# A feed-forward layer whose first tokens are loaded in another order: transposes of 1, 2 and 2 contraction tiles, all issued ahead of the start barrier

## Chip, cores and metric

The kernel runs on one core of a Trainium2 chip. The metric is the device time of one execution in microseconds (us); lower is better. Times are given as the median of several runs; a profile is one further execution, taken by the hardware profiler. All times below are in us unless marked otherwise, and times inside an execution count from its first instruction.

## What is computed

```
B, S, D, F = 1, 2048, 640, 1728          # x, w1, w2 in bf16
h = jnp.einsum("bsd,df->bsf", x, w1)     # contraction over D
h = silu(h)
out = jnp.einsum("bsf,fd->bsd", h, w2)   # contraction over F
```

## The kernel before

Tokens are worked in four chunks of 512 (`SCH`). D = 640 is five contraction tiles of 128 (`DT`), and F = 1728 is 13 blocks of 128 (`FT`) and one of 64. TensorE needs x with the contraction on the partitions, so x comes from memory by DMA transposes into `xT`; a transpose moves one or more contraction tiles of one chunk (`turned`, line 90, named T(k) or T(k,k+1) below after its tiles). w1 comes by plain DMAs into `w1s`. For the first eight blocks (1024 columns), they are slabs: slab k holds contraction tile k (`slab`, line 118, 256 KB). Slab 0 is split: its first five blocks are issued by ScalarE, the rest by SyncE. The remaining columns of w1 are two more DMAs (lines 151 and 152).

The first chunk is worked with the contraction outermost, so that work can begin when only a part of x and w1 is there. The eight PSUM banks hold eight blocks, and a sweep k (`sweep`, line 189) adds contraction tile k to all eight. A block of a sweep is two matmuls of 64 columns (`step`, line 180), which run side by side; below they are called a pair. Sweep k waits for slab k and for the transpose that brings tile k. With sweep 4 (line 207) the banks close one by one and ScalarE applies Silu to each. Then come blocks 8 to 12 of the first chunk, then the other three chunks, then the second product, and the stores. Those later stages are not touched.

Ahead of the real work TensorE runs dummy matmuls on a zeroed tile (`first_dummies`, line 135): 13 of 128 columns and one pair of 64, each over 256 columns.

Each engine starts with a barrier: it announces its arrival, then waits for the others. The helper `early` (line 98) takes instructions out of the place where they were written and puts them ahead of that barrier: with `arrived=False` ahead of the engine's own arrival, otherwise between its arrival and its wait. So what SyncE issues early delays its arrival, and with it what the others do behind their waits. In the kernel before, SyncE issues T(0,1), the rest of slab 0, slabs 1 and 2 and T(2) ahead of its arrival, and slab 3, T(3,4), slab 4, the rest of w1 and the 15 transposes of the later chunks (line 160) behind the barrier. TensorE runs the dummies and sweeps 0 and 1 (`opening`, line 194) between its arrival and its wait. Behind the barrier stand ScalarE's load of the Silu table with a warming activation (line 154) and GpSimd's memset for it (line 141).

SyncE issues everything in the order of the text, on one queue; ScalarE has a queue of its own for its part of slab 0.

Of the kernel before, what the change touches and what calls it, by code (L numbers as in the profile page):

```python
# [9 lines left out]
def bass_standalone__dense_activation_silu__prompt_kernel(  # L10
# [13 lines left out]
    P = 128  # L24
    NB = 8
    BANK = 512
    DT = D // P
    FT = F // P
    FL = F - FT * P
    SCH = 512  # L30
# [8 lines left out]
    pe, act, dve, pool, sp = nc.tensor, nc.scalar, nc.vector, nc.gpsimd, nc.sync  # L39

    with ExitStack() as es:
# [18 lines left out]
        def sem(name):  # L60
            s = es.enter_context(nc.semaphore(name))
            count[s.name if hasattr(s, "name") else name] = 0
            return [s, 0]

        def tick(ins, s, n=1):
            ins.then_inc(s[0], n)
            s[1] += n
            return (s, s[1])

        def wait(eng, *points):  # L70
            for pt in points:
                if pt is None:
                    continue
                s, v = pt
                key = (id(eng), id(s))
                if seen.get(key, 0) < v:
                    eng.wait_ge(s[0], v)
                    seen[key] = v
# [6 lines left out]
        def load(eng, out_ap, in_ap):  # L85
            s = sem(f"s_ld{n_dma[0]}")
            n_dma[0] += 1
            return tick(eng.dma_start(out=out_ap, in_=in_ap), s, 16)

        def turned(c0, c1, k0, k1):  # L90
            s = sem(f"s_tr{n_dma[0]}")
            n_dma[0] += 1
            return tick(sp.dma_start_transpose(
                out=xT[:, k0:k1, c0:c1], in_=xf[c0:c1, k0 * P:k1 * P]), s, 16)

        ET = mybir.EngineType

        def early(emit, engine, arrived=True):
            n = len(nc.main_func.blocks[0].instructions)
            r = emit()  # L100
            lst = nc.main_func.blocks[0].instructions
            new = lst[n:]
            del lst[n:]
            at = next(
                i for i, ins in enumerate(lst)
                if ins.opcode == ("EventSemaphore" if arrived else "Drain") and ins.engine == engine
            )
            lst[at:at] = new
            return r
# [8 lines left out]
        def slab(eng, k, f0=0, f1=NO):  # L118
            return load(eng, w1s[:, k, f0 * P:f1 * P], w1_v[:, k, f0 * P:f1 * P])

        ld_w1 = {}
        ld_t = {}
        ld_t[0] = ld_t[1] = early(lambda: turned(0, SCH, 0, 2), ET.SP, False)
        ld_w1[0] = early(lambda: slab(act, 0, 0, NA), ET.Activation, False)
        p_z = early(lambda: tick(dve.memset(z[:, :], 0.0), s_dve), ET.DVE, False)  # L125

# [2 lines left out]
        def dummies(n, w):  # L129
            for _ in range(n):  # L130
                for c0 in range(0, P, w):
                    pe.matmul(ps[c0:c0 + w, 3, 0:HB], lhsT=z[:, 0:w], rhs=z[:, :],  # L132
                              start=True, stop=True)

        def first_dummies():
            wait(pe, p_z)
            dummies(13, P)
            dummies(1, HC)


        p_warm = tick(pool.memset(warm[:, :], 0.0), s_pool)  # L141

        ld_w1b = early(lambda: slab(sp, 0, NA, NO), ET.SP, False)
        ld_w1[1] = early(lambda: slab(sp, 1), ET.SP, False)
        ld_w1[2] = early(lambda: slab(sp, 2), ET.SP, False)
        ld_t[2] = early(lambda: turned(0, SCH, 2, 3), ET.SP, False)
        ld_w1[3] = slab(sp, 3)
        ld_t[3] = ld_t[4] = turned(0, SCH, 3, DT)
        ld_w1[4] = slab(sp, 4)
        CM = CO + 2 * P  # L150
        ld_rest = load(sp, w1s[:, :, CO:CM], w1_v[:, :, CO:CM])
        ld_rest2 = load(sp, w1s[:, :, CM:F], w1_v[:, :, CM:F])
# [33 lines left out]
        def part(k, ft, c0, c1, start=False, stop=False):  # L186
            return step(ft, k, ft, c0, c1, start, stop)

        def sweep(k, c0, c1, *waits):
            wait(pe, *waits)  # L190
            for ft in range(NO):
                part(k, ft, c0, c1)

        def opening():
            first_dummies()
            wait(pe, ld_t[0], ld_w1[0])
            for ft in range(NO):
                if ft == NA:
                    wait(pe, ld_w1b)
                part(0, ft, 0, SCH, start=True)  # L200
            sweep(1, 0, SCH, ld_w1[1], ld_t[1])

        early(opening, ET.PE)
        for k in range(2, DT - 1):
            sweep(k, 0, SCH, ld_w1[k], ld_t[k])
        wait(pe, ld_w1[4], ld_t[4])
        for ft in range(NO):
# [202 lines left out]
```

## Time and profile before

| | us |
|---|---|
| median of 3 runs | 125.18 |
| lowest, highest | 124.72, 125.32 |
| the profiled execution's own time | 124.39 |
| its span, first to last instruction | 122.9 |
| TensorE busy in the span | 120.4 |
| ScalarE busy | 38.8 |
| VectorE busy | 6.9 |

A line of the profile names a source line (L172 is the helper that issues every real matmul, L132 the dummies), an engine (PE is a TensorE matmul, PEld its weight load, SPq the issuing of a DMA by SyncE), and the tiles written and read. In the order of time, the first two numbers are the start and the length of a group, x the number of instructions in it, and the brackets give the idle time before it and what ended it. The length of a DMA line is only the time that the engine takes to issue it; the DMA view gives the time from issue to landing. Durations of pipelined matmuls overlap: their rate is read from the spacing of their starts.

### The profile page before, as it was taken

To read this page: it belongs to the slowest core of one execution; us is meant where nothing else is said; L and a number is where in the kernel's file an instruction comes from. 1 tells how busy PE (TensorE), PEld (TensorE's weight loads), DVE (VectorE), ACT (ScalarE), POOL (GpSimd) and SP (SyncE) were. 2 spreads that over 40 slices of the span, in tenths; PEclk is the share of its full clock that TensorE was granted. 3 is DMA by queue.
4 is the path that set the end of the run, shared out by engine and by line. 5 is a ranking of instruction groups with operands and counts; after the bars stand their busy time and mean duration, and the time that the engine had idled before them with its cause. 6 is when DMAs were issued, how large, how long until landed. Compare 5 with 4: busy or idle time off the path is not lost.

```text
span 122.9 us, 2298 instructions
## 1 busy us (share of the span) xinstructions
PE 120.4 (98%) x1056; PEld 58.9 (48%) x1057; DVE 6.9 (6%) x11; ACT 38.8 (32%) x67; POOL 0.3 (0%) x5
## 2 busy tenths in 40 slices
PE   8999999999999999999999999999999999999993
PEld 5455555555555555555544444444444444444452
DVE  0000000000000000000000022002101300222001
ACT  0403975555555555555530011002101200110110
POOL 0000000000000000000000000000000000000000
PEclk9999999999999999999999999999999999999999
DMA  7999955465991000000000014202200220022122
GB/s 150 242 217 341 135 122 116 92 84 100 303 392 43 0 0 0 8 0 0 0 0 5 0 25 103 48 0 107 107 0 5 107 107 0 5 107 107 53 75 85
DMA packets 19481, 10.42 MB, mean 85 GB/s; under 512 B 13456, under 2 KB 18960, under 8 KB 19472
## 3 DMA queue, kind: packets, MB, share of 16 engines
q1 hardware_dynamic: 19184, 10.05, 32.3%
q10 hardware_dynamic: 288, 0.23, 0.7%
q8 instruction: 8, 0.13, 0.4%
q14 instruction: 1, 0.01, 0.0%
HBM read 4.51 MB, written 2.62 MB: 58 GB/s over the span
## 4 chain that ended last, share of the span: by engine, by line
PE 98%; issue 0%; ACT 0%; DVEq 0%
PE ps L172 95%; PE ps L132 3%; ACT o_sb L254 0%; DVEq L395 0%
## 5 line engine op out<-in xcount | busy, mean ns | idle before, releaser
L172 PE MATMUL ps<-xT,w1s 128*64 128x512 bf16 x540 | 58.9, 381 | 0.0
L172 PE MATMUL ps<-w2s,hT 64*128 64x512 bf16 (+3 forms) x376 | 46.0, 369 | 0.2 <-issue 0.2
L172 PEld LDWEIGHTS ps<-xT,w1s 128*64 128x64 bf16 x540 | 30.0, 111 | 28.6 <-issue 0.5
L176 ACT ACTIVATE hT<-ps 128x512 bf16<-128x512 f32 x52 | 30.0, 608 | 24.7 <-PE ps L172 24.7
L172 PEld LDWEIGHTS ps<-w2s,hT 64*128 64x128 bf16 (+1 forms) x377 | 21.0, 95 | 24.1 <-issue 0.2
L254 ACT CAST o_sb<-ps 128x512 bf16<-128x512 f32 (+1 forms) x9 | 4.9, 550 | 41.5 <-PE ps L172 41.5
L172 PE MATMUL ps<-hT,w2s 64*128 64x512 bf16 x104 | 11.7, 376 | 0.0
L172 PEld LDWEIGHTS ps<-hT,w2s 64*128 64x128 bf16 x104 | 5.0, 94 | 6.3 <-issue 0.4
L252 DVE CAST o_sb<-ps 128x512 bf16<-128x512 f32 (+1 forms) x8 | 5.4, 674 | 40.5 <-PE ps L172 40.5
L252 DVE CAST oT<-ps 128x512 bf16<-128x512 f32 x2 | 1.4, 692 | 73.3 <-PE ps L172 73.3
L254 ACT CAST oT<-ps 128x512 bf16<-128x512 f32 x2 | 1.2, 585 | 10.6 <-PE ps L172 10.6
L132 PE MATMUL ps<-z 128*128 128x256 bf16 (+1 forms) x15 | 3.3, 419 | 0.4 <-DVE z L125 0.4
L172 PE MATMUL ps<-w2t,hTt 64*128 64x512 bf16 (+2 forms) x17 | 2.9, 364 | 0.0
L154 ACT ACT_TABLE_LOAD x1 | 1.3, 1283 | 4.8 <-DVEq L395 4.8
L132 PEld LDWEIGHTS ps<-z 128*128 128x128 bf16 (+1 forms) x15 | 1.9, 143 | 1.5 <-issue 0.4
L176 ACT ACTIVATE hTt<-ps 128x512 bf16<-128x512 f32 x2 | 1.2, 597 | 1.0 <-PE ps L172 1.0
L172 PEld LDWEIGHTS ps<-w2t,hTt 64*128 64x128 bf16 x17 | 0.9, 94 | 1.1
L172 PE MATMUL ps<-hTt,w2t 64*128 64x512 bf16 x4 | 0.8, 376 | 0.0
L172 PEld LDWEIGHTS ps<-hTt,w2t 64*128 64x128 bf16 x4 | 0.2, 94 | 0.2
L154 ACT ACTIVATE warm<-warm 128x32 f32<-128x32 f32 x1 | 0.2, 229 | 0.0
L125 DVE MEMSET z<- 128x128 uint32 x1 | 0.2, 165 | 0.2 <-issue 0.2
L141 POOL MEMSET warm<- 128x32 f32 x1 | 0.1, 124 | 4.3 <-POOLq L395 4.3
(4 smaller groups left out, 0.4 us busy)
## 6 DMA issues: line engine op xcount, KB each, us to landing
out_dram<-o_sb SPq DMA_DIRECT2D x15, 160.0 KB, 1.8
w2s<-in_w_dram SPq DMA_DIRECT2D x1, 1120.0 KB, 6.4
w1s<-in_w_dram SPq DMA_DIRECT2D x4, 256.0 KB, 3.7
w2s<-in_w_dram SPq DMA_DIRECT2D x1, 960.0 KB, 8.5
w1s<-in_w_dram SPq DMA_DIRECT2D x1, 560.0 KB, 5.4
w1s<-in_w_dram SPq DMA_DIRECT2D x1, 320.0 KB, 4.3
xT<-in_x_dram SPq DMA_TRANSPOSE x18, 3.7
w1s<-in_w_dram ACTq DMA_DIRECT2D x1, 160.0 KB, 2.5
```

The costliest lines, as they stand in the source:

```text
L125: p_z = early(lambda: tick(dve.memset(z[:, :], 0.0), s_dve), ET.DVE, False)
L132: pe.matmul(ps[c0:c0 + w, 3, 0:HB], lhsT=z[:, 0:w], rhs=z[:, :], start=True, stop=True)
L141: p_warm = tick(pool.memset(warm[:, :], 0.0), s_pool)
L154: act.activation(out=warm[:, :], in_=warm[:, :], func=ACT.Silu)
L172: return pe.matmul(o, lhsT=l, rhs=r, start=start, stop=stop, skip_group_check=shared)
L176: r = tick(act.activation(out=out_ap, in_=in_ap, func=ACT.Silu), s_act)
L252: r = tick(dve.tensor_copy(out=out_ap, in_=in_ap), s_dve)
L254: r = tick(act.copy(out=out_ap, in_=in_ap), s_act)
```

## The change

The first transpose brings only tile 0, the second tiles 1 and 2, the third tiles 3 and 4. SyncE issues, all ahead of its arrival: T(0), the rest of slab 0, slab 1, T(1,2), slab 2, T(3,4), slab 3, slab 4. So slab 1 goes ahead of the second transpose, and slab 3 behind the third, where it was ahead of it. TensorE runs sweep 2 too before it waits at the barrier. Of the dummies of 128 columns, 10 are left of 13.

```diff
-        ld_t[0] = ld_t[1] = early(lambda: turned(0, SCH, 0, 2), ET.SP, False)
+        ld_t[0] = early(lambda: turned(0, SCH, 0, 1), ET.SP, False)
...
-            dummies(13, P)
+            dummies(10, P)
             dummies(1, HC)
...
         ld_w1b = early(lambda: slab(sp, 0, NA, NO), ET.SP, False)
         ld_w1[1] = early(lambda: slab(sp, 1), ET.SP, False)
+        ld_t[1] = ld_t[2] = early(lambda: turned(0, SCH, 1, 3), ET.SP, False)
         ld_w1[2] = early(lambda: slab(sp, 2), ET.SP, False)
-        ld_t[2] = early(lambda: turned(0, SCH, 2, 3), ET.SP, False)
-        ld_w1[3] = slab(sp, 3)
-        ld_t[3] = ld_t[4] = turned(0, SCH, 3, DT)
-        ld_w1[4] = slab(sp, 4)
+        ld_t[3] = ld_t[4] = early(lambda: turned(0, SCH, 3, DT), ET.SP, False)
+        ld_w1[3] = early(lambda: slab(sp, 3), ET.SP, False)
+        ld_w1[4] = early(lambda: slab(sp, 4), ET.SP, False)
...
-            sweep(1, 0, SCH, ld_w1[1], ld_t[1])
+            for k in (1, 2):
+                sweep(k, 0, SCH, ld_w1[k], ld_t[k])
 
         early(opening, ET.PE)
-        for k in range(2, DT - 1):
+        for k in range(3, DT - 1):
             sweep(k, 0, SCH, ld_w1[k], ld_t[k])
```

## The prediction

> **What bounds the kernel now.** I read the engine totals first, then the chain that ended last, then the opening in order of time, for SyncE and for TensorE, and last the DMA view over short windows.
>
> ```profile
> PE 120.4 (98%) x1056; PEld 58.9 (48%) x1057; DVE 6.9 (6%) x11; ACT 38.8 (32%) x67; POOL 0.3 (0%) x5
> ...
> PE 98%; issue 0%; ACT 0%; DVEq 0%
> PE ps L172 95%; PE ps L132 3%; ACT o_sb L254 0%; DVEq L395 0%
> ```
>
> TensorE is the chain from end to end: L132 are the dummies, L172 all real matmuls. Behind the opening it never idles, so the end moves by exactly what moves in the opening. The opening in order of time (start, length, engine, in brackets the idle time before and what ended it):
>
> ```profile
> 0.00 1.33 SPq L93 DMA_TRANSPOSE xT<-in_x_dram  x1
> 1.39 1.51 SPq L88 DMA_DIRECT2D w1s<-in_w_dram  x3
> 2.94 1.16 SPq L93 DMA_TRANSPOSE xT<-in_x_dram  x1
> 4.75 0.33 SPq L88 DMA_DIRECT2D w1s<-in_w_dram  x1
> 5.14 1.24 SPq L93 DMA_TRANSPOSE xT<-in_x_dram  x1
> 6.43 1.62 SPq L88 DMA_DIRECT2D w1s<-in_w_dram  x3
> ...
> 0.39 3.31 PE L132 MATMUL ps<-z 128*128 128x256 bf16 x15 [0.39 <-DVE z L125]
> 3.60 0.18 PEld L172 LDWEIGHTS ps<-xT,w1s 128*64 128x64 bf16 x4 [0.20 <-DMA xT<-in_x_dram]
> ...
> 3.60 1.03 PE L172 MATMUL ps<-xT,w1s 128*64 128x512 bf16 x4
> ...
> 4.46 0.60 PE L172 MATMUL ps<-xT,w1s 128*64 128x512 bf16 x4
> ...
> 9.65 10.52 PE L172 MATMUL ps<-xT,w1s 128*64 128x512 bf16 x96
> ```
>
> Real work starts at 3.60, when the first transpose lands. Its first two pairs (the two 64-column halves of a block run together) start at 3.60 and 4.03, the next at 4.46 and 4.68: 0.43 each, then 0.216 (the last row: 48 pairs, (10.52 - 0.38)/47). The clock step lies at about 4.46; only this spacing shows it, as the page's row of granted clock is full from the first slice. So a sweep of 8 pairs costs 1.73, and the sweeps start at 3.60; 4.46 + 6 x 0.216 = 5.76; 7.48; 9.21; 10.94. The first Silu at 11.37 is one matmul after the last of these, so there is no hidden stall.
>
> The landings, issue plus the DMA view's time to landing: T(0,1) 3.6, slab 0's rest 1.39 + 3.6 = 4.99, slab 1 2.01 + 3.6 = 5.61, slab 2 2.47 + 3.8 = 6.27, T(2) 2.94 + 3.9 = 6.84, slab 3 4.75 + 2.8 = 7.55, T(3,4) 5.14 + 3.5 = 8.64, slab 4 6.43 + 3.9 = 10.33. Each is ahead of its sweep, by 0.15 (slab 1) to 0.6.
>
> Why slab 3 took 2.8 and slab 4 3.9 is in the DMA rows. GB/s from 2.8 to 4.4, behind T(0,1); from 7.8 to 9.8, behind T(3,4); from 5.8 to 7.0, behind the single T(2):
>
> ```profile
> GB/s 238 212 225 199 147 192 134 20 58 19 90 58 51 0 0 38 38 19 58 58 96 205 218 154 423 179 294 192 141 154 0 173 70 192 90 365 243 480 224 531
> ...
> GB/s 292 308 308 174 200 118 87 0 82 41 123 82 164 41 123 123 82 123 123 164 174 143 102 195 205 246 123 154 184 215 184 410 215 410 348 358 348 215 348 348
> ...
> GB/s 256 213 86 179 154 60 119 111 34 248 179 171 102 359 154 17 290 154 77 341 273 273 341 205 478 68 410 137 273 341 273 410 478 410 410 273 546 341 171 265
> ```
>
> Behind a two-tile transpose the queue crawls for about a microsecond; behind the single one it is soon at 300 and more. In landings: slab 4 lands 10.33 - 8.64 = 1.7 after the two-tile T(3,4); slab 0's rest and slab 1 land 1.4 and 2.0 after T(0,1); slab 3 lands 0.7 after the single T(2). Data arrive in the order of issue throughout.
>
> **The change, part by part.** First the issue times, with the durations and gaps of before. A single-tile transpose costs 1.16 against 1.24, so the first costs 1.33 - 0.08 = 1.25. Then: slab 0's rest 1.31, slab 1 1.93, T(1,2) 2.39, slab 2 3.68, T(3,4) 4.15, slab 3 5.44, slab 4 5.91 to 6.34. SyncE then arrives; before it took 0.65 from its last early issue (4.10) to its next instruction (4.75), so 6.99. The two remaining slabs of w1 (7.00 before) and the 15 later transposes (8.09) keep their times. Cost 0.
>
> *Waits on SyncE's arrival.* ScalarE's table load goes from 4.75 to 6.99, plus 1.28 and 0.23: ready at 8.5, needed at 11.37. GpSimd's memset (0.12) lies inside that. TensorE meets the barrier after sweep 2, at 9.4 or later. All covered, by 2.4 at least; they would cost only if SyncE came later than that.
>
> *Three dummies fewer, a single first tile.* The dummies end 3 x 0.2135 = 0.64 earlier, at 3.70 - 0.64 = 3.06 (the spacing: two dummies of 256 columns equal one cold pair). T(0) carries 128 KB less: 0.47 at some 280 GB/s and 0.08 of issue, so it lands at 3.05 instead of 3.6. Bounds: 2.7, the shortest landing of any transpose in the trace, and 3.6, no gain. Starting at 3.05, 1.41 is cold: 3.28 pairs, and 4.72 x 0.216 = 1.02 follow. Sweep 0 ends at 5.48, **0.28 ahead** of before. Slab 0's rest is due by 4.8 and comes 0.7 to 1.4 after T(0): hidden.
>
> *T(1,2), due at 5.48.* Before, tiles 0 and 1 came together. Now tile 1 is issued at 2.39 in a two-tile transpose, whose landing took 3.6 and 3.5. It lands at 5.95 (5.9 to 6.3 by the three early rows; slab 1 ahead of it lands 1.3 to 2.0 after T(0), at 4.35 to 5.05, and a two-tile transpose 1.09 after the slab ahead, worked out below: no later than 6.14). Sweep 1 waits 0.47 and starts at 5.95: **+0.19** against 5.76. The early start is spent.
>
> *Slab 2, due at 5.95 + 1.73 = 7.68.* It stands behind a two-tile transpose: + 1.7 gives 7.65, just in time; + 0.7 gives 6.65.
>
> *T(3,4), due at 9.41.* A two-tile transpose lands 1.09 after the slab ahead of it (8.64 - 7.55): 8.74. In time.
>
> *Slab 3, due at 9.41 too.* This is the step I choose as the deciding one. Before it was ahead of T(3,4), behind the single tile; now it is behind T(3,4), in the very place of slab 4. Both ends: + 1.7 gives 10.44, a wait of 1.03; + 0.7 on the short chain (6.65, 7.74) gives 8.44, none. I take 1.7, the row of the same bytes behind the same transpose. Sweep 3 starts at 10.44 instead of 9.21: **+1.23**. Slab 4 follows by some 0.66 (as slab 2 follows slab 1): 11.1, due at 12.17. The rest of w1 and the next 512 tokens keep their issue while TensorE is later: hidden.
>
> The sum: 124.39 (the profiled execution) + 1.23 = **125.6**.
>
> Against the median: the three runs lie 0.33 to 0.93 above the profiled one, and the trace can't show where. In the new kernel the start of sweep 3 is set by the loads from SyncE's first instruction on, so time that TensorE loses ahead of it (a later clock step above all) is absorbed, up to the 1.03 of the wait. Since TensorE never idles behind the opening, I put the runs' extra time there: 125.6 holds for the median too, +0.3% on 125.18. [...]
>
> **The rivals.** *Slower: the wait rides on top.* Place: slab 3 ahead of sweep 3. If the runs' extra 0.79 lies behind the opening or in the loads, nothing absorbs it: 125.18 + 1.23 = 126.4. It decides from the point where slab 3 lands over 0.63 behind the moment at which the kernel before starts sweep 3 in the same run (9.84 against 9.21 in the profiled one). For it: the median lies above the profile, the cause unseen. Against: no idle time behind the opening.
>
> *The queue recovers fast.* If slabs 2 and 3 land 0.7 behind their transposes, only T(1,2) is left: +0.19 with the clock step of the profile, down to -0.28 with a later one: about 125.2. For it: slab 3 of before. Against: both two-tile rows.
>
> *The transposes are quick and the early start stays.* If T(1,2) landed like a slab of its size (2.8, slab 3), at 5.19, and the slabs 0.7 behind, all 0.28 would be kept: 124.9; with a clock step after sweep 0 the whole 0.55: 124.6. Against: 3.5, 3.6 and 3.9 for the early transposes. [...]
>
> *The change doesn't start earlier.* T(0) lands at 3.6 all the same, and TensorE idles from 3.06. That would cost nothing more, since sweep 1 waits for T(1,2).
>
> **How the numbers follow.** The forecast 0.37 (its own range 125.2 to 126.0), with the last rival in it; on top 0.33; fast recovery 0.20; quick transposes 0.10. A measurement of this kernel tells about 0.5% from no change, 0.63 either way: 124.55 to 125.81. Faster is only the far end of the quick case: 0.06. Slower: the case on top and the upper edge of the forecast, 0.38. The same: 0.56. The range from 124.8 to 126.6 leaves out the far ends.
>
> **What would show it.** Right: real matmuls from about 3.05, a wait before sweep 1 for xT until about 5.95, and one before sweep 3 for w1s until about 10.4, with GB/s near 100 for a microsecond behind each two-tile transpose. Wrong: slab 3 landing before 9.4, T(1,2) before 5.5, or the clock step much later than 4.46.

## The result, and the profile after

The changed kernel takes 125.40 us (median of 22 runs, 124.99 to 126.11) against 124.84 (22 runs, 124.45 to 125.37) for the kernel before: a ratio of 1.0047, with a 95% interval of 1.0033 to 1.0062. It is 0.5% slower, just inside the band that the prediction calls the same. The new kernel's profiled execution took 126.11, the longest of its 22; that of before, 124.39, lies below all of its 22 (from 124.45). So the two profiles lie further apart (1.72) than the medians (0.56). The ratios leave out runs more than 1.5% above the fastest of their kernel: 2 of 12 in e10 and 6 of 13 in e11, the one profiled among these, and none elsewhere.

The engine totals and the chain that ended last, of the changed kernel:

```profile
PE 121.1 (97%) x1054; PEld 59.6 (48%) x1054; DVE 7.0 (6%) x11; ACT 38.8 (31%) x67; POOL 0.3 (0%) x5
...
PE 90%; SPq 4%; DMA 4%; issue 0%; ACT 0%
PE ps L171 90%; DMA w1s<-in_w_dram 4%; SPq L93 3%; SPq L88 1%; ACT o_sb L254 0%
```

TensorE is no longer the chain from end to end: 8% of it is now SyncE's issuing and one DMA of w1. The later part of the chain in order of time says which (start, length, what):

```profile
4.31 1.24 SPq L93
5.55 0.04 issue
5.59 5.27 DMA w1s<-in_w_dram
10.86 0.04 issue
10.90 111.82 PE ps L171 x993
```

The DMA issued at 5.59 is slab 3, the first copy behind T(3,4). It lands at 10.86, and sweep 3 starts with it. The opening in order of time:

```profile
0.39 2.67 PE L132 MATMUL ps<-z 128*128 128x256 bf16 x12 [0.39 <-DVE z L125]
1.30 1.03 SPq L88 DMA_DIRECT2D w1s<-in_w_dram  x2
2.38 1.26 SPq L93 DMA_TRANSPOSE xT<-in_x_dram  x1
...
3.06 0.18 PEld L171 LDWEIGHTS ps<-xT,w1s 128*64 128x64 bf16 x4 [0.29 <-DMA xT<-in_x_dram]
3.06 6.59 PE L171 MATMUL ps<-xT,w1s 128*64 128x512 bf16 x48
...
4.77 0.18 PEld L171 LDWEIGHTS ps<-xT,w1s 128*64 128x64 bf16 x2 [0.24 <-issue]
5.20 0.33 PEld L171 LDWEIGHTS ps<-xT,w1s 128*64 128x64 bf16 x4 [0.24 <-issue]
...
5.98 0.60 PEld L171 LDWEIGHTS ps<-xT,w1s 128*64 128x64 bf16 x8 [0.46 <-issue]
...
7.05 1.28 ACT L153 ACT_TABLE_LOAD   x1 [7.05 <-DVEq L395]
10.90 0.62 PE L171 MATMUL ps<-xT,w1s 128*64 128x512 bf16 x4 [1.25 <-DMA w1s<-in_w_dram]
```

Real work starts at 3.06 instead of 3.60. The weight loads 0.43 apart (4.77, 5.20) belong to the pairs ahead of what the prediction calls the clock step, "cold" below: the point where the spacing of the pairs falls from 0.43 to 0.216. Here the step comes at 5.2, not at 4.46. As before, only the spacing shows it: the granted clock is 1.00 on both sides of it, in the kernel before (3.60 to 4.46, 4.46 to 9.20) and in the changed one (3.06 to 5.20, 5.20 to 9.65). So "clock" is my reading; what makes the step isn't shown. Sweep 1 starts at 6.01 (5.76 before), sweep 2 at 7.74 (7.49), sweep 3, behind 1.25 of idle time, at 10.90 (9.22).

One number orders all that follows. The time of the profiled execution less the start of sweep 3 is 124.39 - 9.22 = 115.17 before and 126.11 - 10.90 = 115.21 after. In nine of the experiments that have such a pair below it is 115.18 to 115.24 too. So nothing behind the start of sweep 3 costs more or less in these, and a kernel's time can be read as the start of sweep 3 plus 115.2.

### The profile page after: what moved, and what is told of

It reads as the page before. It is cut to its first block, busy times and chain, and to the rows that moved or that the text cites. A ratio compares the mean times of both kernels' runs of the same rounds, so it can differ in the third digit from the quotient of the medians.

```text
span 124.6 us, 2293 instructions
## 1 busy us (share of the span) xinstructions
PE 121.1 (97%) x1054; PEld 59.6 (48%) x1054; DVE 7.0 (6%) x11; ACT 38.8 (31%) x67; POOL 0.3 (0%) x5
## 4 chain that ended last, share of the span: by engine, by line
PE 90%; SPq 4%; DMA 4%; issue 0%; ACT 0%
PE ps L171 90%; DMA w1s<-in_w_dram 4%; SPq L93 3%; SPq L88 1%; ACT o_sb L254 0%
## 5 line engine op out<-in xcount | busy, mean ns | idle before, releaser
L171 PE MATMUL ps<-xT,w1s 128*64 128x512 bf16 x540 | 59.9, 384 | 1.3 <-DMA w1s<-in_w_dram 1.3
L171 PEld LDWEIGHTS ps<-xT,w1s 128*64 128x64 bf16 x540 | 31.1, 111 | 29.9 <-DMA w1s<-in_w_dram 1.7
L132 PE MATMUL ps<-z 128*128 128x256 bf16 (+1 forms) x12 | 2.7, 419 | 0.4 <-DVE z L125 0.4
```

The costliest lines, as they stand in the source:

```text
L171: return pe.matmul(o, lhsT=l, rhs=r, start=start, stop=stop, skip_group_check=shared)
```

## The experiments

All ratios are to the kernel before, run on the same chip in the same rounds, with 95% intervals. "Step" is the time at which the spacing of the pairs falls from 0.43 to 0.216. The table has the two profiled executions and those of the experiments; e10 and e11, whose profiles are told of last, aren't in it:

| kernel | ratio to before | own time of the profile | sweep 1 / sweep 3 start | step |
|---|---|---|---|---|
| before | 1 | 124.39 | 5.76 / 9.22 | 4.5 |
| changed | 1.0047 [1.0033, 1.0062] | 126.11 | 6.01 / 10.90 | 5.2 |
| e1 slab 3 first | 1.0032 [1.0013, 1.0050] | 125.19 | 6.48 / 10.01 | 6.6 |
| e2 later ones late | 1.0068 [1.0043, 1.0093] | 125.77 | 6.46 / 10.56 | 6.4 |
| e3 before, swapped | 1.0047 [1.0031, 1.0064] | 125.23 | 6.01 / 10.02 | 5.0 |
| e4 13 dummies | 1.0040 [1.0019, 1.0062] | 125.40 | 6.37 / 10.16 | 3.9 |
| e5 before, 10 dummies | 1.0086 [1.0061, 1.0110] | 125.61 | 6.98 / 10.43 | 6.9 |
| e6 slab 3 first, 13 dummies | 1.0027 [1.0005, 1.0049] | 125.17 | 6.51 / 9.96 | 4.5 |
| e7 before, 6 dummies | 1.0121 [1.0086, 1.0156] | 125.47 | 6.84 / 10.29 | 6.5 |
| e8 single tiles | 1.0062 [1.0039, 1.0085] | 125.46 | 6.44 / 9.90 | 4.6 |
| e9 before, 10 and 4 dummies | 0.9993 [0.9972, 1.0014] | 125.21 | 6.54 / 10.00 | 6.1 |
| e12 before, early issue alone | 0.9993 [0.9968, 1.0018] | 124.58 | 5.95 / 9.40 | under 4 |

The theory at the start (A) was that of the prediction: the changed kernel is slower because slab 3 now stands behind T(3,4). Its rivals: the late tile 1 (B), the late arrival at the barrier (C), and for the crawl itself, SyncE's issuing of further transposes (D).

### Slab 3 ahead of T(3,4) again

```diff
-        ld_t[3] = ld_t[4] = early(lambda: turned(0, SCH, 3, DT), ET.SP, False)
         ld_w1[3] = early(lambda: slab(sp, 3), ET.SP, False)
+        ld_t[3] = ld_t[4] = early(lambda: turned(0, SCH, 3, DT), ET.SP, False)
```

> The changed kernel with slab 3 issued ahead of T(3,4); nothing else. Theory A (the cost is the wait for slab 3, which crawls behind the two-tile T(3,4)): slab 3 lands at about 7.9, the wait of 1.25 before sweep 3 goes, and the kernel takes 0.5 to 0.9 less than the changed one, about that of the kernel before (124.84) or up to 0.3 below it; T(3,4) lands near 9.0, due at 9.5, and slab 4 behind it at 10.7 to 11.5, due at 11.2, may wait for 0.3. Theory B (the cost is tile 1, which now comes 2.4 later in a transpose of its own): nothing is gained, 125.4. Theory C (the cost is the late arrival at the barrier): 125.4.

Slab 3 landed at 8.45 and the wait before sweep 3 was gone, as A says. But the gain was small: 1.0032 against 1.0047, with intervals that overlap, where A expected all of it back. A alone doesn't carry the result: with the wait gone, something else holds sweep 3 back to 10.01. In this profile it is the late step, at 6.6. Every pair of sweep 0 ran cold, though nothing waited:

```profile
5.20 0.18 PEld L171 LDWEIGHTS ps<-xT,w1s 128*64 128x64 bf16 x2 [0.25 <-issue]
5.63 0.18 PEld L171 LDWEIGHTS ps<-xT,w1s 128*64 128x64 bf16 x2 [0.25 <-issue]
...
6.48 4.93 PEld L171 LDWEIGHTS ps<-xT,w1s 128*64 128x64 bf16 x46 [0.22 <-issue]
```

### The later transposes held back

```diff
+        wait(sp, ld_w1[3])
         ld_xc = {}
```

> The changed kernel, with SyncE waiting for slab 3 to land before it issues the 15 transposes of the later chunks; it tells why slab 3 lands 2.5 after T(3,4). If copies crawl because the transposes' own writes are still under way (theory A), slab 3 still lands 1.4 to 2.5 behind T(3,4), at 9.8 to 10.9, and the transposes for the second chunk come some 2 later, so that TensorE may wait for them: 125.4 to 127. If they crawl because SyncE is issuing transposes meanwhile (theory D), slab 3 lands 0.7 to 1.0 behind T(3,4), at 9.0 to 9.3, and sweep 3 has no wait.

SyncE issued no transpose between 5.53 and 10.53, and slab 3 still landed 1.9 behind T(3,4) (8.59, 10.51). D falls: slab 3 is late with no further transpose issued. The time, 1.0068, is inside what was expected.

The traces say more of what "late" is. A DMA's semaphore counts to 16 here (the 16 in `load`), and the trace has the time of each count, as if the copy landed in sixteen parts. In all 13 profiles that have T(3,4), the first part of the slab behind it lands 0.5 to 0.65 behind it. What differs is the time from the first part to the last: 0.1 in e12, 0.5 in e4, 1.1 in before, 1.4 in e2, 2.0 in the changed kernel. In e2 fourteen parts of slab 3 were there by 9.27, the next came at 9.55, and the last alone at 10.51. In the changed kernel the first part of slab 4 came at 9.51, ahead of eight parts of slab 3. The DMA rate says the same; for the changed kernel, from 7.6 to 11.0 in slices of 0.085:

```profile
GB/s 250 166 112 96 120 145 72 120 96 72 145 169 145 193 265 217 289 337 319 331 325 289 314 277 259 289 277 307 337 265 331 325 349 313 325 331 360 352 328 352
```

It is under 200 from 7.7, ahead of T(3,4)'s landing, to 8.8, and then 217 to 360, while slab 3 still needs until 10.86. So behind T(3,4) the whole queue isn't slow for all of that time: parts of a copy fall behind while others run ahead to the next one. What in the chip makes them fall behind stays open; that it is the transpose's own writes was argued, not shown.

### Slab 3 and T(3,4) swapped in the kernel before

```diff
-        ld_w1[3] = slab(sp, 3)
         ld_t[3] = ld_t[4] = turned(0, SCH, 3, DT)
+        ld_w1[3] = slab(sp, 3)
```

> The kernel before, with slab 3 and T(3,4) changing places, both behind the barrier as before; nothing else. Theory A: T(3,4) lands at about 8.0 to 8.3 and slab 3 at 1.7 to 2.5 behind it, 9.7 to 10.8, due at 9.2: slower than the kernel before by 0.4 to 1.3, 125.3 to 126.1. Theories B and C: tile 1 and the barrier are as before, so 124.84 within 0.2.

1.0047, or 0.6 more, inside what A expected: T(3,4) landed at 8.18, slab 3 at 9.98. The chain of this kernel and the wait:

```profile
6.04 3.94 DMA w1s<-in_w_dram
9.98 0.04 issue
10.02 111.82 PE ps L172 x993
```

So the deciding step of the prediction, taken alone, costs as much as the whole change.

### 13 dummies in the changed kernel

```diff
-            dummies(10, P)
+            dummies(13, P)
```

> The changed kernel with 13 dummies of 128 columns instead of 10, so that real work starts 0.6 later, at about 3.65. Theory A: sweep 1 can't start before T(1,2) lands at 5.9 and sweep 3 not before slab 3, so the early start is worth nothing: within 0.15 of the changed kernel, 125.4. If the early start does reach the end (theory E, the waits matter less than the rate at the start), it is slower by about 0.3, 125.7.

1.0040 against 1.0047: no difference that can be told. In its profile the step came at 3.9 and sweep 0 was through by 5.4, but sweep 1 waited until 6.37 for T(1,2), and slab 3 came at 10.12. The early start is worth nothing that these runs can tell, as A expected.

### Fewer dummies in the kernel before

```diff
-            dummies(13, P)
+            dummies(10, P)
```

That is e5. e7 has 6; e9 has 10 and, for the one pair of 64 columns, four.

> The kernel before with 10 dummies of 128 columns instead of 13; real work still starts when T(0,1) lands, at about 3.55, after some 0.5 of idle time. Put here because the spacing of the pairs shows the clock step at 3.9 to 5.1 in the three kernels with 13 dummies so far (before, the swap of slab 3 and T(3,4), and the changed kernel with 13) and at 5.2 to 6.6 in the three with 10. Theory F (fewer dummies and the gap behind them delay the clock step): the step comes at 5.2 to 6.6 and the kernel is slower than before by 0.3 to 0.8. Rival G (the step's time is chance, the same for both): the same as before within 0.15.

> The kernel before with 6 dummies of 128 columns instead of 13: TensorE idles for about 1.4 between them and the real work at 3.55. Theory F: the clock step comes later than with 10, at 6 to 8, and the kernel is slower than before by 0.8 to 1.7. Rival G: within 0.2 of before.

> The kernel before with 10 dummies of 128 columns and 4 pairs of 64 columns instead of 13 and 1: the same time of dummies as before, no idle time ahead of the real work at 3.6, but fewer of the full ones. With 10 and 1 and the idle time of 0.6 the clock step came at 6.9 and the kernel took 0.99 more than before. Theory F1 (the idle time delays the step): as before within 0.2, step at 3.9 to 5.1. Rival F2 (the number of full dummies matters): step at 5.2 to 6.9, slower by 0.4 to 1.1.

Three and seven dummies fewer cost 0.9% and 1.2%, and three fewer cost nothing when shorter ones fill the time: in these three it is the idle time ahead of the real work that costs, not the number of full dummies. With 10 dummies, the wait (0.62 for the matmuls, 0.91 for the weight loads) and the cold pairs behind it:

```profile
3.68 0.18 PEld L172 LDWEIGHTS ps<-xT,w1s 128*64 128x64 bf16 x4 [0.91 <-DMA xT<-in_x_dram]
3.68 8.00 PE L172 MATMUL ps<-xT,w1s 128*64 128x512 bf16 x58 [0.62 <-DMA xT<-in_x_dram]
...
6.24 0.18 PEld L172 LDWEIGHTS ps<-xT,w1s 128*64 128x64 bf16 x2 [0.25 <-issue]
...
6.67 4.74 PEld L172 LDWEIGHTS ps<-xT,w1s 128*64 128x64 bf16 x44 [0.25 <-issue]
```

Pairs still start 0.43 apart until 6.67. But the pattern that led to these runs, an early step with 13 dummies and a late one with 10, was partly chance: in the gapless e9 the step of the one profile is at 6.1 too, at a median equal to before's. One profile doesn't give a kernel's step; the ratios say what the steps cost. Nor does idle time always bring a late step: in the profile of e10, below, TensorE idles for 1.07 ahead of the real work, and the eight pairs of sweep 0 are then 0.22 to 0.24 apart from the first on:

```profile
4.34 1.44 PEld L173 LDWEIGHTS ps<-xT,w1s 128*64 128x64 bf16 x16 [1.37 <-DMA xT<-in_x_dram]
4.34 8.93 PE L173 MATMUL ps<-xT,w1s 128*64 128x512 bf16 x80 [1.07 <-DMA xT<-in_x_dram]
```

In the changed kernel the dummies end at 3.06, when the real work starts, so there is next to no idle time to fill, and the three dummies more of e4 bought nothing that can be told.

### Slab 3 first and 13 dummies

> The changed kernel with slab 3 ahead of T(3,4) and with 13 dummies. No wait for slab 3 is left; T(1,2) lands at 6.0 to 6.2. Theory F: the clock step comes at 3.9 to 5.1, sweep 1 waits for T(1,2), starts at 6.1 to 6.3 and the kernel is 0.2 to 0.4 above before (124.9 to 125.1), under the 125.19 of the same kernel with 10. Rival G: real work starts later by 0.4 with the same clock step, so 125.2 to 125.4.

1.0027: neither distinguishable from e1 nor free of the loss. The step came early, at 4.5, as F expected, but the time, 0.45 above before, is that of G. The profile shows what is left, tile 1:

```profile
2.38 1.25 SPq L93 DMA_TRANSPOSE xT<-in_x_dram  x1
6.51 5.34 PE L171 MATMUL ps<-xT,w1s 128*64 128x512 bf16 x47 [0.62 <-DMA xT<-in_x_dram]
```

T(1,2), issued at 2.38, lands at 6.37; sweep 0 was through by 5.7. That fits theory B.

### The early issue alone

```diff
-        ld_w1[3] = slab(sp, 3)
-        ld_t[3] = ld_t[4] = turned(0, SCH, 3, DT)
-        ld_w1[4] = slab(sp, 4)
+        ld_w1[3] = early(lambda: slab(sp, 3), ET.SP, False)
+        ld_t[3] = ld_t[4] = early(lambda: turned(0, SCH, 3, DT), ET.SP, False)
+        ld_w1[4] = early(lambda: slab(sp, 4), ET.SP, False)
```

This is the kernel before with that and with sweep 2 ahead of TensorE's wait.

> The kernel before, in its order and with its 13 dummies, with one part of the change alone: SyncE issues slab 3, T(3,4) and slab 4 ahead of its arrival, and TensorE runs sweep 2 ahead of its wait. It separates what is left, 0.27%, of the changed kernel with slab 3 first and 13 dummies, which differs from this one only in how the five tiles are split. Theory B (tile 1 comes too late in a transpose of its own with tile 2): the remainder goes, within 0.15 of the kernel before. Theory C (the late arrival costs): the remainder stays, 0.2 to 0.5 slower than before.

0.9993: C falls, the late arrival costs nothing that can be told. e12 and e6 differ in the split of the five tiles, with the second transpose ahead of slab 2 in e6 and behind it in e12, and in nothing else. The loss of 0.27% goes with the split, but barely clear of the noise: the intervals, from 1.0005 in e6 and up to 1.0018 in e12, overlap. B is the likely second cause; the waits for T(1,2) in the profiles of e4 and e6 speak for it.

### Single tiles, and an early start in another way

```diff
+        ld_t[3] = early(lambda: turned(0, SCH, 3, 4), ET.SP, False)
         ld_w1[3] = early(lambda: slab(sp, 3), ET.SP, False)
+        ld_t[4] = early(lambda: turned(0, SCH, 4, 5), ET.SP, False)
```

> The changed kernel with T(3,4) split into two transposes of one tile: T(3), slab 3, T(4), slab 4. Theory A (the crawl comes behind a two-tile transpose, and is short behind a single one): T(3) lands at about 7.9 and slab 3 0.7 to 1.0 behind it, 8.6 to 8.9, ahead of sweep 3, so the wait goes and the kernel takes what the version with slab 3 first takes, 125.2. If the crawl is the same behind any transpose: slab 3 lands 1.7 to 2.5 behind T(3), at 9.6 to 10.4, and the kernel takes 125.3 to 125.5.

Slab 3 landed 1.1 behind T(3), at 9.32, later than the 8.6 to 8.9 expected but in time for a sweep 3 that started at 9.90. The kernel took 1.0062 and not the 125.2 expected: one more issue of a transpose puts the later ones back, and TensorE now waits for the second chunk, which is why its time less the start of sweep 3 is 115.56:

```profile
19.11 1.70 PE L172 MATMUL ps<-xT,w1s 128*64 128x512 bf16 x14 [0.17 <-DMA xT<-in_x_dram]
```

The last two kept the order of before and gave the rest of slab 0 to ScalarE's queue (`slab(act, 0, NA, NO)`), one of them with T(0) and T(1) as two transposes and 11 dummies.

> The kernel before with T(0) and T(1) as two transposes, one right behind the other, the rest of slab 0 issued by ScalarE behind its first part, and 11 dummies of 128 columns: an early start without a late tile 1. T(0) lands at 3.0 to 3.2, T(1), issued at 1.3, at 4.0 to 4.3, the rest of slab 0 by 4, slab 1 (issued at 2.55) at 4.9 to 5.6, slab 2 by 6.3, T(2) (issued at 3.5) at 6.6 to 7.3. If all are in time (sweep 1 due at 5.5, sweep 2 at 7.2), 0.1 to 0.3 under the kernel before; if the two streams hold each other up and slab 1 or T(2) is late, 0.1 to 0.5 above.

> The kernel before with the rest of slab 0 issued by ScalarE; nothing else. SyncE's later issues come 0.6 earlier. In the profiled execution of before nothing waited, so theory A expects no difference, within 0.15; if part of the runs of before do wait in the opening (slab 1 is only 0.15 ahead of its sweep in the profile), 0.1 to 0.3 faster.

Ratios of 1.0029 [0.9992, 1.0066] and 1.0005 [0.9978, 1.0033]: no gain. The first is no single value: of the ten runs behind it, seven lie at 124.63 to 124.86 and three at 126.30 to 126.44. In its profile T(0) landed at 4.30, where 3.0 to 3.2 was expected. In the one profile of e11, where nothing but the queue of that copy was changed, T(0,1) landed at 4.23; in the six others with T(0,1) first and the copy on SyncE's queue it landed at 3.46 to 3.67. So the second copy on ScalarE's queue goes with a later first transpose; why was not tried. No version here beats the kernel before.

## Why the prediction was right, step by step

**The forecast, 125.6,** stands against 125.40. Its ground, one wait for slab 3 that takes the place of what the early start gains, is what the chain after shows, and e3 shows that this wait alone costs as much as the whole change; but the wait is not the only cause, and two of its sizes were off. That the number came so close is in part luck. The forecast of +0.3% stood on 125.18, the median of three runs of before; over 22 runs that median is 124.84, so 125.6 is 0.6% above it, and 0.5% was measured. And the profile of the changed kernel, which the sum was built for, took 126.11, not 125.6.

**Issue times and barrier.** Predicted 2.39 for T(1,2), 4.15 for T(3,4), 5.44 for slab 3, measured 2.38, 4.31, 5.59: slab 2, behind T(1,2), took 0.58 to issue, not 0.43. The table load went to 7.05 (6.99 predicted) and cost nothing, as e12 shows.

**The early start.** T(0) landed at 3.02 (3.05 predicted), real work began at 3.06. That it would be spent by sweep 1 was right: 6.01 (5.95 predicted). In the profile most of it was spent on the step, which came at 5.2 and not at the 4.46 that I carried over; T(1,2), landing at 5.88, added only some 0.16. In e4 and e6, where the step was early, sweep 1 did wait for T(1,2), for 0.8 and 0.6 by the idle time of the matmuls (0.95 and 0.8 counted as the 0.16 is, by when the next pair was due). Two causes with one effect: whichever comes last sets sweep 1.

**The term that was mis-sized: 1.7 for a slab behind a two-tile transpose.** Slab 2 took 1.4, slab 3 2.5 (8.33 to 10.86). T(3,4) came earlier than predicted (8.33, not 8.74), which balanced half of it: 10.86 against 10.44. Over the profiles here the first slab of 256 KB behind a two-tile transpose lands 0.7 (e12, slab 4) to 2.5 behind it, 1.6 in the middle; behind a single one 0.6 to 1.3. I had taken one row as a constant; it is a spread, and its long end is in the profile of the changed kernel. The sign that the prediction gave, about 100 GB/s for a microsecond behind each two-tile transpose, came only in part: behind T(3,4) the rate is over 200 again after 0.5, and slab 3 is late because its parts land up to 2.0 apart. Nor was each load of before only 0.15 to 0.6 ahead of its sweep, as the prediction has it: that holds for the later of the two that a sweep needs. Slab 3 itself was 1.6 ahead (7.59 against 9.22), and this is what moving it behind T(3,4) used up.

**Absorption.** The profiles differ by 1.72, the medians by 0.56. By time = start of sweep 3 + 115.2, the median run starts sweep 3 at 9.64 before and at 10.19 after. So the typical run of before is 0.4 later than its profile, and 126.4, the figure of the rival "on top", fell. That the wait absorbs what TensorE loses ahead of it, as the prediction counted on, shows in e3: its nine runs spread over 0.43 (125.14 to 125.57), the 30 of before beside them over 1.30. In the changed kernel it isn't shown: its lowest, median and highest runs lie 0.54, 0.56 and 0.74 above those of before, so the spread is no narrower; a landing of slab 3 that varies from run to run would hide it, but those runs have no trace. Nor have those of before, so where a typical one loses its 0.4 is argued too; the steps at 3.9 to 6.9 in these profiles make the step the likely place, which is my estimate. Before and e9, whose dummies both end at 3.70, have it at 4.5 and 6.1, 1.6 apart; that it moves from run to run of one kernel isn't shown, as each kernel has one trace.

**The rivals.** Fast recovery (125.2) happened in single profiles (e12, e6: slab 4 0.7 and 0.9 behind T(3,4); e4, in the order of the changed kernel: slab 3 1.0 behind), not in the one profile of the changed kernel. Quick transposes fell: T(1,2) took 3.5, T(3,4) 4.0. The swap of slab 3 alone (e3) costs 0.47%, and the split without it (e6 against e12, 0.27% against -0.07%) probably some 0.3%; together they make 0.47%, which is less than the sum. A wait at sweep 3 that takes in what is lost ahead of it would give this, but the intervals are too wide to show it.

## What to carry to other kernels

When work is consumed in the order of loads, an earlier first load gains only as much as the second and third come earlier too (here the first transpose landed at 3.02 instead of 3.6, and the kernel took 0.47% more): write down the landing and the due time of every one, not of the first. Put a copy that is due together with a transpose ahead of the transpose in the queue; in the kernel before that was worth 0.47% (e3). Waits in a row on one engine need not add up (here 0.47% and probably some 0.3% alone, 0.47% together; that the later one takes in what the earlier one cost is my estimate); so parts of a change must be undone one at a time and together, and one profile doesn't stand for the median.

## What was not expected of the hardware

Idle time of 0.6 and 1.5 between the dummies and the real work cost 0.86% and 1.21% (1.1 and 1.5), though the real work began at 3.68 and 3.71 instead of 3.60: in both profiles the step came later, at 6.9 and 6.5 against 4.5. Filling 0.6 of it with small matmuls on zeros avoided the cost (0.9993), though in the one profile of e10 the step had come before 4.34 in spite of 1.07 of idle time. And a plain copy behind a DMA transpose on one queue lands 0.6 to 2.5 behind it, for the same 256 KB; behind T(3,4) its first part always lands within 0.65, and what varies, from 0.1 to 2.0, is how far apart its parts land.
